# First backward steps of an attention-block gradient kernel: a V tile, the first dK, rows of e, the dw4 stores and some side jobs in other places

## The chip, the cores and the metric

The kernel runs on one core of one Trainium2 chip. The metric is the device time of one execution in microseconds (us). A core has a matrix engine (PE, with its weight loads shown as PEld), a vector engine (DVE), a scalar engine (ACT), GpSimd (POOL) and a queue engine (SP). They run side by side, each in its own program order, and wait for each other by semaphores. Transfers between HBM and on-chip memory are issued here from SP (nearly all loads), from POOL (all stores but a few at the end) and from ACT (small loads of rows of e); they share 16 DMA engines.

## What is computed

Forward and backward pass of one transformer block at decode: one token, attention over a cache of 8192 keys for 32 heads of 192, then a small MLP, each modulated by a vector from `c @ w_mod`. The kernel returns the output and the gradients of nine inputs. Cut to what matters:

```python
def attn(x, k, v, wq, wo):                  # 32 heads, 8192 keys, head size 192
    q = x @ wq
    p = softmax(q . k * 192**-0.5)
    return (p . v) @ wo
def mlp(x, w1, w2, w3, w4):                 # one token: only x, w3 and w4 matter
    x1 = x + hs
    return x1 + gelu(layernorm(x1) @ w3) @ w4
h = layernorm(x) * (1 + ca) + sa;  x = x + ga * attn(h, K, V, wq, wo)
h = layernorm(x) * (1 + cb) + sb;  x = x + gb * mlp(h, ...)
# outputs: x and the gradients of x, K, V, wq, wo, w3, w4, c, w_mod
```

K and V are 100 MB each in bfloat16 and so are their gradients dK and dV. Each row of dV is p times the gradient dO of a head's output, and each row of dK is dS times q, where dS comes from p and from dP, the products of dO with the rows of V. K is read once (forward), V twice (forward for the output, backward for dP), and dK and dV are written once.

## The kernel before

**Stages.** A forward loop over the heads loads K and V in tiles of 128 partitions x 32 rows x 192 (1536 KB, half a head) and leaves e (unnormalised p) in `E_all`, and transposed rows of e in DRAM (`eT_d`). The code after the loop handles the last head, the MLP forward and its backward down to `dao_bf`, the gradient at the attention output. Then come 64 backward steps `s` (L1363), one for each half head, from the last head down.

**Tiles.** Five tiles `KB` (names KX, KY, KC, KD, KE at L353) held K in the forward pass. In the backward pass the list `OB` (L354) gives them in turn to dV and dK: step `s` writes dV to `OL[2s]` and dK to `OL[2s+1]` (L1293). So dV of step 0 is in KC, dK of step 0 in KY, dV of step 1 in KX, dK of step 1 in KE, and so on round. Three tiles `VB` hold V; the V tile of step 0 was loaded to KY, those of steps 1 to 3 to VB2, VB0 and VB1 (`v_buf`, L1290) before the backward pass begins. The V tile of step 4 goes to VB2 again.

**One backward step.** DVE multiplies the V tile of the next step by dO, half a tile at a time (`mul_q`, L1035). PE sums the products with an identity matrix into `dot_ps` (`tree_q`, L1056), DVE reduces that to dP (`dot_sum`, L344) and forms dS. DVE multiplies dS by q, in two halves (`dk_part`, L1072), and POOL issues the store of dK (`dk_store`, L1322). For dV, PE forms the outer products of rows of e (`er_b`, loaded by `load_er`, L995) and dO in eight groups (`dv_groups`, L1067), ACT copies each from PSUM to the dV tile (L1068), and POOL issues the store (`dv_store`, L1318). SP loads the V tile of step s+4 as soon as the second half product of step s+1 has freed its tile (L1407). In steps 0 and 1 PE also forms dq from K tiles that are still there (`dq_rows`, `dq_cols`), and DVE waits for it before it starts dK.

**Before step 0.** A prelude (L1325 to L1360) does dV of step 0 and the products for steps 0 and 1. The gradient of w4 (dw4) is 12 blocks of 128x640, each the product of a broadcast row with a column (`dw4_dve` on DVE, `dw4_act` on ACT). Four blocks go to KX on DVE and are stored; five more go to another part of KX (three on DVE, two on ACT) and are stored; three go to the staging tile `stg0` on ACT and are stored. Three small pieces of work on DVE, kept in `late0` (L1362), run in step 0.

**Side jobs.** The gradients of wo, w3, wq and w_mod are cut into pieces (generators `g_do`, `g_dwo`, `g_ld`, `g_dw3`, `g_dq` and others). The list `jobs` (L1245) holds them in order, and `slot()`, called four times in a step, runs about one piece a call from step 6 on. `g_ld` loads a wo tile, `g_do` transposes it in two pieces and forms dO of two heads in the third, `g_dwo` overwrites it with the gradient and stores it. `g_dw3` forms rows of the gradient of w3 in the staging tile `stg` (a single buffer, so it waits for the store before) and stores them; the last one also loads the first wq chunk, over the tile from which `g_dw3` reads. `g_rest(3)` is three empty pieces.

**Order.** PE, DVE, ACT and SP run in an order that a planner fixes from the program's order (L355 and the `manual_schedule` blocks); POOL runs in the program's order.

Of the kernel before, what the change touches and what calls it, by code (L numbers as in the profile page):

```python
# [20 lines left out]
def kernel(  # L21
# [28 lines left out]
    D = A_x.shape[-1]  # L50
# [75 lines left out]
    def mean_sum(ps, groups, name):  # L126
        m = tcol(groups, name)
        V_.reduce_sum(out=m, in_=ps[:, 0 : groups * ND].rearrange("p (a b) -> p a b", b=ND), axis=AX.X)
        return m
# [187 lines left out]
    def flat(kb):  # L317
        return kb.rearrange("p j d -> p (j d)")


    NVB = 3
# [29 lines left out]
    H1 = HQ - 1  # L351
    TL = NT - 1
    KX, KY, KC, KD, KE = (KB[(2 * HQ + k) % NKB] for k in (-4, -5, -3, -2, -1))  # L353
    OB = (KC, KY, KX, KE, KD)  # L354
    NVA = (7 * JQ) // 16  # L355
    MO = 256
    with tc.tile_pool(name="vs", bufs=3) as vsp, tc.tile_pool(name="ft", bufs=2) as ft, \
# [85 lines left out]
        def mp_out(h, mp):  # L443
            A_.copy(out=M1[:, h, :], in_=mp[:, 0:MW])
            mt = ft.tile([P, MW], FP32, name="mt", bufs=1)
            A_.copy(out=mt[64:128, :], in_=mp[64:128, MO : MO + MW])
            return mt
# [8 lines left out]
        def m_add(h, mp, mt):  # L456
            t, b = divmod(h, 2)
            V_.tensor_tensor(out=M2[64 * b : 64 * b + 64, t, :], in0=mp[0:64, MO : MO + MW], in1=mt[64:128, :], op=ALU.add)
# [56 lines left out]
        with tc.manual_schedule(engines=ORDER):  # L515
# [297 lines left out]
            def w3t(n=1):  # L813
                for _ in range(n):
                    next(w3t_it, None)
# [56 lines left out]
            w3t()  # L872
            pe.pop(0)()
            w3t()
            dw4_v = out_7.rearrange("(a p) r -> p a r", p=P)

            def dw4_dve(dst, a0, lo, hi):
                for a in range(lo, hi):
                    V_.tensor_scalar(out=dst[:, (a - a0) * D : (a - a0 + 1) * D], in0=dbo_bc, scalar1=g_[:, a : a + 1], scalar2=None, op0=ALU.mult)

            def dw4_store(dst, lo, n):
                nc.gpsimd.dma_start(out=dw4_v[:, lo : lo + n, :], in_=dst[:, 0 : n * D].rearrange("p (a r) -> p a r", a=n))
# [24 lines left out]
                    T_.matmul(h2_ps[:, k : k + 1], lhsT=w4r(a)[:, k * P : (k + 1) * P], rhs=g_bf[:, a : a + 1], start=(a == 0), stop=(a == NF - 1))  # L907
            do_t(TL, 0)
            do_t(TL, 8)
            mt = mp_out(H1 - 1, mp)  # L910

            def dw4_act(dst, a0, lo, hi):
                for a in range(lo, hi):
                    A_.activation(out=dst[:, (a - a0) * D : (a - a0 + 1) * D], in_=dbo_bc, func=ACT.Copy, scale=g_[:, a : a + 1])

            dn_ps = psO.tile([P, 256], FP32, name="dn_ps", tag="op")[:, 0:ND]
            for k in range(ND):
                for a in range(NF):
                    T_.matmul(dn_ps[:, k : k + 1], lhsT=w3T(a, k), rhs=du_bf[:, a : a + 1], start=(a == 0), stop=(a == NF - 1))

            sk = mean_sum(ps5, 5, "sk")
            w6 = col(6 * ND, "w6").rearrange("p (a b) -> p a b", b=ND)
            A1, Ag, B1, Bg, uu, vv = (w6[:, k, :] for k in range(6))
# [6 lines left out]
            NWg = col(4 * ND, "NWg").rearrange("p (a b) -> p a b", b=ND)  # L930
            V_.tensor_scalar(out=NW, in0=NW, scalar1=rho[:, 0:1], scalar2=None, op0=ALU.mult)
            V_.tensor_copy(out=bo, in_=h2_ps[:, 0:ND])
            dw4_dve(flat(KX), 0, 0, 2)
            pr = col(4 * ND, "pr").rearrange("p (a b) -> p a b", b=ND)
            V_.tensor_tensor(out=pr, in0=dn_ps[:, None, :].to_broadcast([P, 4, ND]), in1=G, op=ALU.mult)
            ps = mean_mm(pr.rearrange("p a b -> p (a b)"), 4 * ND)
# [14 lines left out]
            V_.reduce_sum(out=qr, in_=q4.rearrange("p a b -> p b a"), axis=AX.X)  # L951
            V_.tensor_tensor(out=dao_bf, in0=vg, in1=qr, op=ALU.add)
            V_.tensor_copy(out=d_n2, in_=dn_ps)
            m_add(H1 - 1, mp, mt)
            dw4_dve(flat(KX), 0, 2, 4)
            dw4_store(flat(KX), 0, 4)

            def dx1_out():
                q = pr
# [38 lines left out]
    def ht(s):  # L998

        return H1 - s // 2, (1 - s % 2 if s < 2 else s % 2)  # L1000
# [46 lines left out]
    def half_q(s, q):  # L1047
        if halved(s, q):
            V_.tensor_tensor(out=pq[:, q, :, 0:HW], in0=pq[:, q, :, 0:HW], in1=pq[:, q, :, HW:DH], op=ALU.add)
# [63 lines left out]
    def g_do(n):  # L1113
        do_t(TL - n, 0)
        yield
        do_t(TL - n, 8)
        yield
        assert done_s[0] >= 4 * (n - NDR + 1)
        do_mm(TL - n)
        done.add(n)  # L1120
        yield
# [62 lines left out]
    def g_dwo(n):  # L1184
        t = TL - n
        w = wo_l.pop(t)
        for k in range(3):
            V_.tensor_scalar(out=w[:, k, :], in0=dao_bc, scalar1=o_col[:, 3 * t + k : 3 * t + k + 1], scalar2=None, op0=ALU.mult)
        nc.gpsimd.dma_start(out=dwo_v[t], in_=w)
        yield  # L1190

    def g_rest(n):
        for _ in range(n):
            yield
# [21 lines left out]
    def g_dw3(lo, n):  # L1216
        dw3_v = out_6.rearrange("(i p) n -> p i n", p=P)
        o3 = bst.tile([P, ND, CW], BF16, name="stg").rearrange("p a r -> p (a r)")
        for i in range(n):
            V_.tensor_scalar(out=o3[:, i * F : (i + 1) * F], in0=du_bc, scalar1=n2[:, lo + i : lo + i + 1], scalar2=None, op0=ALU.mult)  # L1220
        nc.gpsimd.dma_start(out=dw3_v[:, lo : lo + n, :], in_=o3[:, 0 : n * F].rearrange("p (a r) -> p a r", a=n))
        if lo + n == ND:
            next_w()
        yield
# [26 lines left out]
    late = list(range(GX, NWM))  # L1251
    for n in range(NT):
        if n + 3 < NT:
            jobs.append((3, g_do(n + 3)))
            if n < 2:
                jobs.append((1, g_dw3(2 * n + 2, 2 - n)))
            jobs.append((1, g_dwo(n + 3)))
        if n + 4 < NT:
            jobs.append((1, g_ld(n + 4)))
        if n == 1:  # L1260
            jobs.append((3, g_rest(3)))
        if n > 0:
            jobs.append((5, g_dq(TL - n + 1)))
            if n % 2 == 1:
                wseq.append((wq_v, (TL - n + 1) // 2))
        if n % 4 == 0 and n > 0 and late:
            wseq.append((wm_v, late[0]))
            jobs.append((10, g_wm(late.pop(0))))
# [19 lines left out]
            prog[1] += 1  # L1288

    def v_buf(s):  # L1290
        return KY if s == 0 else VB[(s + 1) % NVB]

    OL = [OB[i % 5] for i in range(2 * NS - 5)]  # L1293
    OL += [v_buf(NS - 3), OB[3], v_buf(NS - 2), OB[4], v_buf(NS - 1)]
# [36 lines left out]
    do_mm(TL, 0)  # L1331
    mul_q(0, 1)
    half_q(0, 1)
    dv_groups(dV0, er, doh, (4,))
    tree_q(ps, 0, 0, 0, 6)
    dv_groups(dV0, er, doh, (6,))
# [13 lines left out]
    T_.matmul(c_ps, lhsT=c32, rhs=cs, start=True, stop=True)  # L1350
    dv_groups(dV0, er, doh, (5, 7))
    dv_store(0, dV0, JQ, JH)
    dw4_dve(flat(KX)[:, 4 * D :], 4, 4, 7)
    dw4_act(flat(KX)[:, 4 * D :], 4, 7, 9)
    dw4_store(flat(KX)[:, 4 * D :], 4, 5)
    dw4_act(stg0[:, 2 * D :], 9, 9, 12)
    dw4_store(stg0[:, 2 * D :], 9, 3)
    V_.scalar_tensor_tensor(out=cpr, in0=c_ps, scalar=32.0, in1=rinv, op0=ALU.mult, op1=ALU.mult)
    V_.memset(dha, 0.0)
    V_.memset(dsc, 0.0)  # L1360
# [2 lines left out]
    for s in range(NS):  # L1363
        h, t = ht(s)
        nxt = s + 1 < NS
        doh = do_of(h)
        qh = qs_bc[:, h * DH : (h + 1) * DH]
        dP = tcol(JH, "dP")
        dot_sum(ps, dP)
        dS4 = bst.tile([P, JH, 4], BF16, name="dS4", bufs=2)  # L1370
        V_.scalar_tensor_tensor(
            out=dS4,
            in0=dP[:, :, None].to_broadcast([P, JH, 4]),
            scalar=cpr[:, h : h + 1],
            in1=E_all[:, h, t * JH : (t + 1) * JH, None].to_broadcast([P, JH, 4]),
            op0=ALU.subtract,
            op1=ALU.mult,
        )
        dV, dK = OL[2 * s], OL[2 * s + 1]
        gs = [0, 1, 2, 3, 4, 5, 6, 7]  # L1380
        if not nxt:
            gs = [0, 2, 4, 6, 1, 3, 5, 7]
        if s == 0:
            gs = [None] * 8
        else:
            er = er_l.pop(s)
        if nxt:
            ps = psR.tile([P, JH, TS], FP32, name="dot_ps")

        def dv(k):  # L1390
            if gs[k] is not None:
                dv_groups(dV, er, doh, (gs[k],))

        def tree(q, lo, hi):
            if nxt:
                tree_q(ps, s + 1, q, lo, hi)

        dv(0)
        dv(1)
        slot()  # L1400
        tree(0, 0, 4)
        if nxt:
            mul_q(s + 1, 1)
            half_q(s + 1, 1)
            v_l.pop(s + 1, None)
        if s + 4 < NS:
            v_l[s + 4] = load_v(*ht(s + 4), v_buf(s + 4))  # L1407
        dv(2)
        tree(0, 4, 8)
        dv(3)  # L1410
        tree(0, 8, 12)
        if row is not None:
            dq_cols(row)
            row = None
        dk_part(dK, qh, dS4, 0, JQ)
        if not nxt:
            dv_store(s, dV, 0, JQ, nc.sync)
            dk_store(s, dK, 0, JQ)
        slot()
        dv(4)  # L1420
        tree(1, 0, 3)
        dk_part(dK, qh, dS4, JQ, JH)
        while late0:
            late0.pop(0)()
        dk_store(s, dK, 0 if nxt else JQ, JH)
        dv(5)
        tree(1, 3, 6)
        slot()
        dv(6)
        tree(1, 6, 9)  # L1430
        dv(7)
        if s + 2 < NS:
            er_l[s + 2] = load_er(s + 2)
        if s == 0:
            pass
        elif nxt:
            dv_store(s, dV, 0, JH)
        else:
            dv_store(s, dV, JQ, JH, nc.sync)
        tree(1, 9, 12)  # L1440
        if h == H1:
            row = dq_rows(t, (KD, KE)[t], dS4)
        if s + 2 < NS:
            assert (s + 2) // 4 in done
            mul_q(s + 2, 0)
            half_q(s + 2, 0)
        done_s[0] = s + 1
        slot()
# [33 lines left out]
```

## Time and profile before

| what | us |
|---|---|
| median of 3 runs (1411.46 to 1414.79) | 1413.57 |
| the profiled execution | 1412.54 |
| its span, first to last instruction | 1410.8 |
| PE busy | 1182.7 (84%) |
| DVE busy | 1112.0 (79%) |
| ACT busy | 902.5 (64%) |
| POOL busy | 106.0 (8%) |
| mean rate of all transfers over the span | 404 GB/s |
| HBM read and written | 340.95 MB and 226.43 MB |

Times in the text are from the start of the profiled span. A line of the timeline gives the start, the duration, the engine, the line of the program, the operation with its tiles (buffer numbers left out, so KB is any of the five) and a count; in square brackets stands the idle time before it and what ended it. A line of the stretches gives the busy time of PE, PEld, DVE, ACT and POOL in that stretch with the number of instructions, then the granted clock of PE as a share of full speed, the mean busy share of the 16 DMA engines, and the rate. SPq and ACTq are DMA issues. Matmuls overlap, so a busy PE is not PE at its peak.

### The profile page before, as it was taken

How to read it: one execution, taken by the hardware profiler on the slowest of the kernel's cores; microseconds unless marked ns; L12 is line 12 of the kernel's file. 1: busy time of each engine (PE TensorE's matmuls, PEld its weight loads, DVE VectorE, ACT ScalarE, POOL GpSimd, SP SyncE). 2: the span in 40 equal slices, each digit the busy share in tenths (PEclk: the TensorE clock that was granted, in tenths of full speed). 3: DMA queues.
4: the chain of work that ended last, by engine and by line, in shares of the span. 5: the costliest groups of instructions: out<-in, count | busy, mean ns of one | idle time of the engine just before them, and what ended most of it. 6: DMA issues, size and time to landing. Idle time of an engine off the chain costs nothing.

```text
span 1410.8 us, 30413 instructions
## 1 busy us (share of the span) xinstructions
PE 1182.7 (84%) x12680; PEld 745.5 (53%) x12680; DVE 1112.0 (79%) x1461; ACT 902.5 (64%) x1971; POOL 106.0 (8%) x191
## 2 busy tenths in 40 slices
PE   3988989999998999797867998896877799878965
PEld 2777777777777778443323444443443344334421
DVE  4989999999999998886755875776775777868765
ACT  0767777777777778565545666665655476546654
POOL 0000000000000000110100111101110111101110
PEclk7899999999999999665555555556556555555555
DMA  9999999999999997599999999999999999999998
GB/s 375 389 398 419 418 416 423 411 422 417 418 415 415 408 416 291 209 365 427 424 388 424 427 422 426 421 425 425 425 421 425 414 413 426 419 404 396 424 369 373
DMA packets 76200, 569.36 MB, mean 404 GB/s; under 512 B 7294, under 2 KB 25038, under 8 KB 35998
## 3 DMA queue, kind: packets, MB, share of 16 engines
q1 hardware_dynamic: 51162, 342.03, 59.4%
q0 software_dynamic: 24384, 224.87, 38.3%
q8 instruction: 99, 1.62, 0.4%
q10 hardware_dynamic: 516, 0.51, 0.1%
q14 instruction: 39, 0.32, 0.1%
HBM read 340.95 MB, written 226.43 MB: 402 GB/s over the span
## 4 chain that ended last, share of the span: by engine, by line
issue 58%; DMA 17%; PE 9%; DVE 9%; POOL 5%; ACT 1%; SPq 0%; POOLq 0%; DVEq 0%; ACTq 0%
DMA KB<-in_A_k_cache_dram 7%; DVE prod L330 4%; DMA out_dram<-KB 3%; DMA w_st<-in_A_wq_dram 3%; PE mp L402 2%; DVE prod L334 2%; PE dot_ps L1056 2%; POOL out_dram L1322 2%; POOL out_dram L1318 2%; DMA out_dram<-w_st 2%; DMA stg<-in_A_wq_dram 2%; PE half_ps L340 2%; DMA out_dram<-stg 1%; PE mp L407 1%; PE dv_ps L1067 1%
## 5 line engine op out<-in xcount | busy, mean ns | idle before, releaser
L1068 ACT CAST KB<-dv_ps 128x768 bf16<-128x768 f32 x512 | 397.5, 805 | 164.1 <-PE dv_ps L1067 156.6
L1056 PE MATMUL dot_ps<-pq,ident_bf 128*128 128x256 bf16 x1494 | 380.3, 398 | 22.5 <-DVE dP L344 20.2
L1072 DVE TENSOR_TENSOR KB<-qs_bc,dS 128x3072 bf16<-128x3072 bf16 x122 | 210.7, 1753 | 131.8 <-DMA out_dram<-KB 124.6
L387 ACT ACTIVATE vs<-VB,Ef 128x192 bf16<-128x192 bf16 x840 | 303.5, 447 | 0.0
L1056 PEld LDWEIGHTS <-ident_bf 128*128 128x128 bf16 x1494 | 150.4, 124 | 177.6 <-issue 137.8
L1067 PE MATMUL dv_ps<-do_r,er_b 1*128 1x192 bf16 x2048 | 231.1, 337 | 9.5 <-ACT KB L1068 6.5
L1037 DVE TENSOR_TENSOR pq<-VB,do_r 128x3072 bf16<-128x3072 bf16 x126 | 220.4, 1749 | 15.4 <-PE dot_ps L1056 15.4
L330 DVE TENSOR_TENSOR prod<-KB,qs_bc 128x6144 bf16<-128x6144 bf16 x62 | 207.9, 3353 | 25.5 <-DMA KB<-in_A_k_cache_dram 19.8
L402 PE MATMUL mp<-vs,KB 128*128 128x193 bf16 x1984 | 191.2, 249 | 4.2 <-ACT vs L387 3.3
L402 PEld LDWEIGHTS <-KB 128*128 128x128 bf16 x1984 | 170.4, 98 | 13.3 <-DMA KB<-in_A_k_cache_dram 5.3
L894 ACT COPY wT<-wT_ps 128x1024 bf16<-128x1024 bf16 x82 | 79.1, 965 | 120.4 <-PE wT_ps L893 115.5
L1067 PEld LDWEIGHTS <-er_b 1*128 1x128 bf16 x2048 | 69.6, 104 | 161.1 <-issue 157.9
L340 PE MATMUL half_ps<-prod,ident_bf 128*128 128x256 bf16 x744 | 95.1, 279 | 44.2 <-DVE prod L334 44.1
L380 DVE TENSOR_TENSOR vs<-VB,E 128x1728 bf16<-128x1728 bf16 x120 | 123.7, 1052 | 0.3 <-ACT vs L387 0.3
L334 DVE TENSOR_TENSOR prod<-prod 128x3072 bf16<-128x3072 bf16 x62 | 108.7, 1754 | 1.0
L407 PE MATMUL mp<-vs,KB 128*64 128x193 bf16 x1976 | 107.2, 252 | 0.0
L340 PEld LDWEIGHTS <-ident_bf 128*128 128x128 bf16 x744 | 72.9, 100 | 62.4 <-issue 53.4
L344 DVE TENSOR_REDUCE dP<-dot_ps 128x32 f32<-128x512 f32 x64 | 44.0, 687 | 59.7 <-PE dot_ps L1056 59.5
L407 PEld LDWEIGHTS <-KB 128*64 128x64 bf16 x1976 | 80.1, 110 | 20.1 <-issue 19.7
L367 ACT ACTIVATE E<-S_h,negm 128x256 bf16<-128x256 f32 x31 | 15.8, 508 | 114.9 <-DVE negm L538 112.6
L1322 POOL DMA_DIRECT2D out_dram<-KB x61 | 33.6, 551 | 488.2 <-DVE KB L1072 300.4
L422 PE MATMUL op<-vs,ones_bf 128*32 128x193 bf16 x1920 | 62.1, 250 | 0.0
(359 smaller groups left out, 972.0 us busy)
## 6 DMA issues: line engine op xcount, KB each, us to landing
VB<-in_A_v_cache_dram SPq DMA_DIRECT2D x123, 1536.0 KB
out_dram<-KB POOLq DMA_DIRECT2D x123, 1536.0 KB, 16.1
KB<-in_A_k_cache_dram SPq DMA_DIRECT2D x64, 1536.0 KB
wo_st<-in_A_wo_dram SPq DMA_DIRECT2D x31, 480.0 KB
w_st<-in_A_wq_dram SPq DMA_DIRECT2D x12, 960.0 KB
out_dram<-wo_st POOLq DMA_DIRECT2D x16, 480.0 KB, 16.3
out_dram<-w_st POOLq DMA_DIRECT2D x7, 960.0 KB, 20.6
w_st<-in_w_mod_dram SPq DMA_DIRECT2D x6, 960.0 KB
```

The lines of the kernel that those rows point to most:

```text
L330: V_.tensor_tensor(out=prod, in0=src, in1=vec[:, None, :].to_broadcast([P, JH, DH]), op=ALU.mult)
L334: V_.tensor_tensor(out=prod[:, :, 0:HW], in0=prod[:, :, 0:HW], in1=prod[:, :, DH - HW : DH], op=ALU.add)
L340: T_.matmul(ps, lhsT=ident_bf, rhs=prod[:, :, k : k + TF], start=(k == 0), stop=(k == w - TF))
L380: V_.tensor_tensor(out=vs[:, 0:n, 0:DH].rearrange("p j (a b) -> p j a b", b=4), in0=v[:, v0 : v0 + n, :].rearrange("p j (a b) -> p j a b", ...
L387: A_.activation(out=vs[:, k, 0:DH], in_=v[:, v0 + k, :], func=ACT.Copy, scale=Ef[:, j0 + k : j0 + k + 1])
L402: T_.matmul(mp[:, 0:MW], lhsT=kb[:, j0 + k, 0:P], rhs=vs[:, k, 0:MW], start=(q == 0 and k == 0), stop=(z and k == JQ - 1), skip_group_chec ...
L407: T_.matmul(mp[p0 : p0 + 64, MO : MO + MW], lhsT=kb[:, j0 + k, P:DH], rhs=vs[:, k, 0:MW], start=False, stop=(z and k >= JQ - 2), skip_grou ...
L1037: V_.tensor_tensor(out=pq[:, q], in0=v_l[s][:, q * JQ : (q + 1) * JQ, :], in1=do_of(ht(s)[0])[:, None, :].to_broadcast([P, JQ, DH]), op=AL ...
L1056: T_.matmul(ps[:, q * JQ : (q + 1) * JQ, :], lhsT=ident_bf, rhs=pq[:, q, :, k : k + TS], start=(k == 0), stop=(k == w - TS), skip_group_ch ...
L1067: T_.matmul(ps[:, b, k * DH : (k + 1) * DH], lhsT=er[p0 : p0 + 1, 2 * m + k, :], rhs=doh[p0 : p0 + 1, :], start=True, stop=True)
L1068: A_.copy(out=dV4[:, 2 * q : 2 * q + 2, m * PW : (m + 1) * PW], in_=ps[:, :, 0:PW])
L1072: V_.tensor_tensor(out=dK[:, lo:hi, :].rearrange("p j (a b) -> p j a b", b=4), in0=qh.rearrange("p (a b) -> p a b", b=4)[:, None, :, :].to ...
```

## The change

- `OB`: the second of the five output tiles is VB2 in place of KY. So dK of step 0 is written to VB2, and VB2 goes round among the output tiles. KY takes VB2's place among the V tiles: the V tile of step 4 is loaded to KY, and its load is issued in the prelude, after the second half product of step 0, no longer in step 0's body after the second half product of step 1.
- `mp_out` and `m_add` of the next-to-last head (two copies on ACT, one addition on DVE) are done sooner. They are among the last readers and writers of tiles in whose memory `er_b` comes to lie, so the first load of rows of e waited for the addition.
- dw4: six blocks on DVE, all in KX (three before `pr`, three after `d_n2`), in one store; six blocks on ACT, all in `stg0`, in one store. Three stores become two, and DVE does six blocks in place of seven.
- `late0`: one piece in each of steps 1, 2 and 3, not all three in step 0.
- side jobs: `g_dw3(2, 2)` and `g_dw3(4, 1)` each three pieces sooner; with the latter goes the load of the first wq chunk. `g_rest(3)` now stands between them and `g_do(4)`, so `g_do(4)` comes four pieces later, and `g_dwo(4)` and the wo load `g_ld(5)` three pieces later. The number of pieces is the same.

```diff
-    OB = (KC, KY, KX, KE, KD)
+    OB = (KC, VB[2], KX, KE, KD)
...
             w3t()
             pe.pop(0)()
             w3t()
+            mt = mp_out(H1 - 1, mp)
...
             do_t(TL, 0)
             do_t(TL, 8)
-            mt = mp_out(H1 - 1, mp)
...
+            m_add(H1 - 1, mp, mt)
             sk = mean_sum(ps5, 5, "sk")
...
-            dw4_dve(flat(KX), 0, 0, 2)
+            dw4_dve(flat(KX), 0, 0, 3)
...
             V_.tensor_copy(out=d_n2, in_=dn_ps)
-            m_add(H1 - 1, mp, mt)
-            dw4_dve(flat(KX), 0, 2, 4)
-            dw4_store(flat(KX), 0, 4)
+            dw4_dve(flat(KX), 0, 3, 6)
+            dw4_store(flat(KX), 0, 6)
...
         if n + 3 < NT:
-            jobs.append((3, g_do(n + 3)))
             if n < 2:
                 jobs.append((1, g_dw3(2 * n + 2, 2 - n)))
+            if n == 1:
+                jobs.append((3, g_rest(3)))
+            jobs.append((3, g_do(n + 3)))
             jobs.append((1, g_dwo(n + 3)))
         if n + 4 < NT:
             jobs.append((1, g_ld(n + 4)))
-        if n == 1:
-            jobs.append((3, g_rest(3)))
...
     def v_buf(s):
-        return KY if s == 0 else VB[(s + 1) % NVB]
+        return KY if s == 0 else VB[2] if s == 1 else (VB[1], KY, VB[0])[s % 3]
...
     half_q(0, 1)
+    v_l[4] = load_v(*ht(4), v_buf(4))
...
     dv_store(0, dV0, JQ, JH)
-    dw4_dve(flat(KX)[:, 4 * D :], 4, 4, 7)
-    dw4_act(flat(KX)[:, 4 * D :], 4, 7, 9)
-    dw4_store(flat(KX)[:, 4 * D :], 4, 5)
-    dw4_act(stg0[:, 2 * D :], 9, 9, 12)
-    dw4_store(stg0[:, 2 * D :], 9, 3)
+    dw4_act(stg0, 6, 6, 12)
+    dw4_store(stg0, 6, 6)
...
-        if s + 4 < NS:
+        if 0 < s < NS - 4:
             v_l[s + 4] = load_v(*ht(s + 4), v_buf(s + 4))
...
-        while late0:
+        if s > 0 and late0:
             late0.pop(0)()
```

## The prediction

> **What bounds the kernel now.** I read the 40 slices of the page, then stretches around the turn from forward to backward, the chain of waits, and the timelines of the engines there.
>
> ```profile
> DMA  9999999999999997599999999999999999999998
> GB/s 375 389 398 419 418 416 423 411 422 417 418 415 415 408 416 291 209 365 427 424 388 424 427 422 426 421 425 425 425 421 425 414 413 426 419 404 396 424 369 373
> ```
>
> The transfers bound nearly all of it; one hole stands in slices 16 to 18 (529 to 635 us).
>
> ```profile
> 574.00:584.00 10.00, 8.59 (x57) 4.47 (x58) 9.83 (x17) 6.55 (x10) 0.54 (x1) 0.50 0.38 145
> 584.00:602.00 18.00, 12.42 (x103) 7.50 (x101) 12.68 (x23) 8.25 (x12) 2.79 (x4) 0.59 0.94 357
> 602.00:608.00 6.00, 5.97 (x67) 3.38 (x66) 4.97 (x5) 3.82 (x7) 1.08 (x2) 0.50 0.72 301
> 608.00:618.00 10.00, 7.94 (x71) 4.32 (x70) 6.79 (x8) 8.36 (x14) 1.07 (x2) 0.94 0.98 374
> 618.00:640.00 22.00, 21.36 (x134) 8.42 (x135) 18.49 (x18) 14.52 (x19) 2.68 (x5) 0.53 1.00 386
> 640.00:720.00 80.00, 55.17 (x350) 24.09 (x351) 50.27 (x59) 39.16 (x54) 9.50 (x17) 0.54 1.01 425
> 724.00:726.00 2.00, 2.00 (x14) 0.85 (x15) 2.00 (x3) 1.99 (x3) 0.20 (x1) 0.50 0.77 324
> ```
>
> The last columns are granted clock, DMA share and rate. From 640 transfers are the limit; before 618 computing decides when they can start. By windows of 2 us the missing shares from 574 to 618 add up to 9.7 us (2 x (1 - share) each): 7.4 before 586, 1.9 to 608, 0.4 after. Moving computing sooner pays only in as far as it fills these.
>
> ```profile
> 585.59 10.96 DMA out_dram<-KB
> 605.95 1.40 PE dq_ps L1304 x26
> ```
>
> In the chain, a store of KB (the second dw4 store) is followed by PE's work of step 1: that store sets the pace.
>
> ```profile
> 572.25 1.14 SPq L995 DMA_DIRECT2D er_b<-eT_d  x2
> 584.93 9.93 SPq L325 DMA_DIRECT2D VB<-in_A_v_cache_dram  x2
> ...
> 575.13 0.82 PE L1067 MATMUL dv_ps<-do_r,er_b 1*128 1x192 bf16 x8 [2.37 <-DVE pq L1037]
> 581.15 0.97 DVE L879 TENSOR_SCALAR KB<-w4b,g__10304 128x640 bf16<-128x640 bf16 x3
> 588.16 0.16 DVE L1362 SCALAR_TENSOR_TENSOR du<-t__10307,d_g 128x12 f32<-128x12 f32 x1
> 590.09 1.75 DVE L1037 TENSOR_TENSOR pq<-VB,do_r 128x3072 bf16<-128x3072 bf16 x1
> 596.65 2.24 ACT L1068 CAST KB<-dv_ps 128x768 bf16<-128x768 f32 x3 [6.32 <-DMA out_dram<-KB]
> 597.50 0.50 PE L1067 MATMUL dv_ps<-do_r,er_b 1*128 1x192 bf16 x4 [2.60 <-ACT KB L1068]
> 616.26 0.53 POOL L1322 DMA_DIRECT2D out_dram<-KB  x1 [9.40 <-DVE KB L1072]
> 719.82 1.04 PE L893 MATMUL wT_ps<-ident_bf,wo_st 128*128 128x128 bf16 x8 [13.00 <-DMA wo_st<-in_A_wo_dram]
> ```
>
> **The chain to the store of dK of step 2 (616.26), term by term.**
>
> *Moved out of the way.* ACT's two copies of `mp` (0.34 + 0.32) fall into its idle 1.23 before 568.07; without that cover the wT copies, done at 569.89, still have 1.9 until do_ps starts. On DVE the addition (0.35) and a third dw4 block (0.34) come before `pr`, where DVE waits 0.57 for dn_ps: 0.12 late. Afterwards three blocks (0.97) replace the addition and two (1.03). Taken: 0.
>
> *Rows of e.* The first load then waits for the last matmul of dn_ps, near 569.9, in place of the addition that ended at 572.18. It took 2.9 from issue to PE's start at 575.13, so it lands near 572.8 and dO, ready at 573.23, decides. PE's first tree needs the halved product (DVE, 576.01), so at most 1.2 of it arrives there (577.24), at least 0. Taken: 0.8, near the middle of the higher part, since PE has its groups behind it by then; c_ps (581.41 to 581.88) ends at 581.1.
>
> *Three dw4 blocks less on DVE at 581.15.* They took 0.97. Without them DVE is free at 581.24, and with c_ps at 581.1 the next operation (cpr, 582.04) starts at 581.3: -0.75. Were c_ps not sooner, it would be -0.1.
>
> *late0.* 590.09 - 588.16 = 1.93 leaves step 0. The reduction to dP at 591.76 comes 0.75 + 1.93 = 2.7 sooner; PE's tree before it, ended at 588.2, is 0.75 sooner too and stays ahead. It returns as 0.1 in step 1, 0.8 in step 2 and 1.1 in step 3, each behind that step's dK.
>
> *KX.* ACT's 6.32 before dV of step 1 was the store issued at 585.59, landing after 11.0. Now KX's only store leaves at 573.2; the four blocks took 3.7 to land there, in an emptier queue. For six the bounds are 3.7 and 11.0, so 584.2 at the latest, and ACT comes there at about 588.7 (PE's first groups of step 1, 589.16, less the 0.75). ACT's sixth block (0.74) is covered by its idle 1.83 before 589.28. PE's 2.60 goes: -2.6.
>
> Sum: 0.75 + 1.93 + 2.6 = 5.3 sooner. Step 2's dK is stored near 611.
>
> *The tiles.* VB2 is free for dK of step 0 when the second product of step 1 is done, just before on DVE. Five output and three V tiles remain: 0 from then on.
>
> *The transfers.* SP idles from 573 on, so the V load moves from 584.93 to about 577.7, 7.2 sooner, into the hole: 1.57 MB, 3.7 at 425 GB/s. The second dw4 store, six blocks on ACT from 583.0, leaves at 587.5 (583.0 + 6 x 0.745), as before (587.74), and dK of step 0 behind it on POOL's queue (588.54) too. What nothing fills is the time before the V load (about 2) and before that dw4 store (some 2.5): about 4.7 stays of 9.7, with the lag of some 1.4 from an issue to a rising share. So transfers allow 5.0 and computing 5.3. Some waste will stay between: I take 4.7, bounds 0.5 (below) and 5.3.
>
> **The side jobs.** At 706.8 PE waits 13.0 for the wo tile loaded just ahead of `g_do(4)`. With four pieces between (a step, about 13) that wait goes. The DMA share falls short by 0.96 at 722 to 726, after it. Bounds: 0, and 3.0 if all of 720 to 740 (356 and 367 GB/s) rose to 425. Taken: 0.7.
>
> The price is a new wait. `g_dw3(2, 2)` needs the single `stg`, whose store was issued at 674.34 and lands after 19.8, at 694.1; DVE now reaches the piece near 688.6 and waits up to 5.5. Behind it stand a product, so PE's tree and the next V load on SP, and dK. `g_dw3(4, 1)` may meet the same with its own predecessor: up to 6. They cost only what runs dry: a dK or dV store lands 16.1 after its issue and needs 3.7 itself, so 12.4 are queued, and the 13.0 wait above cost 0.96. Bounds 0 and 11.5; taken 0.4. The wq chunk (960 KB, 2.3) goes ahead of one V load on SP, and wo loads later; V is loaded three steps ahead, so nothing. PE's 8.6 wait for that chunk at 753 goes, under a share of 1.0: nothing.
>
> Sum: 4.7 + 0.7 - 0.4 = 5.0. Span 1410.8 - 5.0 = 1405.8; the profiled execution is 1.74 above its span, and the median 1.03 above that: 1413.57 - 5.0 = 1408.6.
>
> **The clock.** PE's work is priced at the granted clock of these rows, about 0.53. The Trainium skill's page TensorE: Matmul & The Clock Gate, Part 1, says that a busy window of about 3.4 us brings the full clock; with PE's gap closed, step 1 would run at 1.0. Here it does not hold: 618 to 640 PE is 97% busy at 0.53. By the rule PE would gain some 5 more, but the transfers cap it: 1408.3 against 1408.6.
>
> **Rivals.**
>
> *PE's pace takes it back.* 608 to 618 ran at a clock of 0.94 with 5.94 of PE work; sooner, it may get 0.53, where it takes 10.5, 4.6 more, partly under the wait for dq_c; say 3. And PE is the limit from 618 to 640 (21.36 of 22), so late0's 1.9 in steps 2 and 3 may come back. Then 5.3 - 4.8 = 0.5 stays of the chain: 1413.57 - 0.5 - 0.3 = 1412.8. For it: the full clock came just there. Against it: from 618 the DMA share is 1.0, so there the pace is not PE's alone.
>
> *Slower: the staging tile.* If the two waits for `stg` in `g_dw3` (5.5 and 6) run the queues dry, 11.5 - 4.7 - 0.7 = 6.1 is lost: 1419.7. It decides from where a wait exceeds the 12.4 queued, or both fall together. For it: V loads stop with DVE. Against it: the 13.0 wait cost 0.96.
>
> *More.* All of the dip at 720 to 740 goes: 4.7 + 3.0 = 7.7, 1405.9. Against it: small rows of w3 and wq go there anyway.
>
> That the change leaves the er load where it was is possible too (another wait ends last); it takes 0.8 of the forecast at most and stays in its range.
>
> **Chances.** Forecast 0.61 (own range 1407.0 to 1410.7), more 0.10, PE's pace 0.17, staging tile 0.12. About 0.2% (2.8 us) is what a measurement can tell here. Faster 0.71, same 0.17, slower 0.12. The range leaves out the slower case and some of "more": 1405.0 to 1414.0.
>
> **What would show it.** Right: er_b issued near 570; a V load near 577.7; no ACT wait for a store before dV of step 1; dP of step 1 near 589, dK of step 2 stored near 611; DMA share over 0.9 from 602 to 608; no wait of PE for wo_st near 710. Wrong: a clock near 0.5 in step 2 with that store after 614; DVE waiting over 5 at L1220 with a DMA share under 0.9 behind it; or a saving at 640 that is lost by 760.

## The result, and the profile after

The changed kernel takes 1406.81 us (median of 9 runs, 1403.01 to 1410.15), the kernel before on the same chip 1412.49 (9 runs, 1409.40 to 1415.95). The ratio is 0.996 with an interval of 0.9944 to 0.9977: 5.7 us less. The forecast was 5.0 us less, 1408.6.

The profiled executions differ by only 2.4 us (1412.54 and 1410.14), because the forward part, whose program is the same, happened to run 3.3 us longer in the second. So from here on times are also given from a common mark: the start of DVE's operation that writes `du_bf` (L869), with which the MLP backward begins. It starts at 567.44 before and at 570.74 after; from it to the end of the span it is 1410.8 - 567.44 = 843.36 and 1408.4 - 570.74 = 837.66, 5.7 less. To compare a time of after with one of before, take 3.3 off.

The DMA share and the rate in 40 slices, from the page of after:

```profile
DMA  9999999999999998599999999999999999999998
GB/s 375 396 393 419 419 405 419 416 419 417 422 413 416 400 408 327 202 386 427 421 420 425 426 424 421 421 425 412 426 417 424 417 419 414 404 412 391 423 396 355
```

The low pair of shares 7 5 (slices 16 and 17) is now 8 5, and the low rate of slice 21 (388) is 420.

Stretches of after that answer to those of before, each 3.3 us later; the last columns are granted clock, DMA share and GB/s:

```profile
577.30:587.30 10.00, 8.85 (x57) 4.63 (x53) 9.83 (x14) 7.24 (x11) 1.13 (x3) 0.50 0.78 246
587.30:605.30 18.00, 16.98 (x167) 10.28 (x166) 15.78 (x16) 12.60 (x18) 2.45 (x4) 0.59 0.95 360
605.30:611.30 6.00, 5.58 (x40) 2.88 (x38) 1.70 (x4) 3.69 (x7) 0.00 (x0) 0.73 1.02 432
611.30:621.30 10.00, 8.34 (x59) 3.69 (x56) 9.83 (x16) 6.47 (x10) 1.61 (x3) 0.53 0.96 403
...
727.30:729.30 2.00, 2.00 (x18) 1.01 (x17) 0.01 (x1) 1.74 (x4) 0.00 (x0) 0.83 1.05 435
```

The first stretch goes from a share of 0.50 to 0.78 (145 to 246 GB/s), the third from 0.72 to 1.02 (301 to 432), and the last, the dip behind PE's long wait, from 0.77 to 1.05. PE's busy time in 18 us rises from 12.42 to 16.98: most of its idle time in step 1 is gone. Summed as in the prediction (2 us windows, 2 x (1 - share)), from 6 to 74 us after the mark 10.9 us were missing before and 5.3 are after.

The timelines of after, around the same places:

```profile
573.13 1.12 SPq L995 DMA_DIRECT2D er_b<-eT_d  x2
581.23 0.35 SPq L325 DMA_DIRECT2D KB<-in_A_v_cache_dram  x1
...
576.80 0.82 PE L1067 MATMUL dv_ps<-do_r,er_b 1*128 1x192 bf16 x8 [0.51 <-ACT do_r L1021]
592.46 0.68 DVE L344 TENSOR_REDUCE dP<-dot_ps 128x32 f32<-128x512 f32 x1
592.23 1.50 ACT L1068 CAST KB<-dv_ps 128x768 bf16<-128x768 f32 x2
594.10 1.61 ACT L1068 CAST KB<-dv_ps 128x768 bf16<-128x768 f32 x2 [0.37 <-PE dv_ps L1067]
596.38 0.16 DVE L1313 TENSOR_TENSOR dq_x<-dq_c,dq_x 128x1 f32<-128x1 f32 x1 [1.19 <-PE dq_c L1312]
600.47 0.53 POOL L1322 DMA_DIRECT2D out_dram<-KB  x1 [8.01 <-DVE KB L1072]
609.85 0.16 DVE L1313 TENSOR_TENSOR dq_x<-dq_c,dq_x 128x1 f32<-128x1 f32 x1 [4.25 <-PE dq_c L1312]
614.24 0.53 POOL L1322 DMA_DIRECT2D out_dram<-KB  x1 [10.52 <-DVE pr L960]
...
692.20 1.15 DVE L1220 TENSOR_SCALAR stg<-w4b,nQ 128x1536 bf16<-128x1536 bf16 x2 [5.28 <-DMA out_dram<-stg]
721.12 1.04 PE L894 MATMUL wT_ps<-ident_bf,wo_st 128*128 128x128 bf16 x8 [3.26 <-DMA wo_st<-in_A_wo_dram]
758.17 1.03 PE L894 MATMUL wT_ps<-ident_bf,wo_st 128*128 128x128 bf16 x8 [7.03 <-DMA wo_st<-in_A_wo_dram]
```

Rows of e leave at 569.83 on the clock of before. ACT's copies of dV of step 1 (592.23, 594.10) wait for PE at most; the 6.32 for a store is gone. dK of step 1 is stored 29.73 after the mark (36.18 before), dK of step 2 43.50 after it (48.82 before). PE's 13.00 for the wo tile has become 3.26 and, one tile later, 7.03 (10.3 together), and DVE waits 5.28 for the store of `stg`.

### The profile page after: what moved, and what is told of

It is laid out like the page before. It is cut to its first block, busy times and chain, and to the rows that moved or that the text cites. A ratio compares the mean times of both kernels' runs of the same rounds, so it can differ in the third digit from the quotient of the medians.

```text
span 1408.4 us, 30414 instructions
## 1 busy us (share of the span) xinstructions
PE 1184.5 (84%) x12680; PEld 746.2 (53%) x12680; DVE 1111.7 (79%) x1460; ACT 903.4 (64%) x1972; POOL 104.9 (7%) x190
## 3 DMA queue, kind: packets, MB, share of 16 engines
q0 software_dynamic: 24368, 224.87, 38.4%
## 4 chain that ended last, share of the span: by engine, by line
issue 30%; DMA 25%; DVE 22%; PE 17%; POOL 4%; ACT 1%; SPq 0%; POOLq 0%; DVEq 0%
DMA KB<-in_A_k_cache_dram 11%; DVE prod L330 8%; DVE prod L334 4%; PE mp L402 3%; PE dot_ps L1056 3%; DMA stg<-in_A_wq_dram 3%; DMA w_st<-in_A_wq_dram 3%; DMA out_dram<-KB 3%; DVE vs L380 2%; PE half_ps L340 2%; DMA w_st<-in_w_mod_dram 2%; PE mp L407 2%; DVE pq L1037 2%; PE dv_ps L1067 2%; POOL out_dram L1322 1%
## 5 line engine op out<-in xcount | busy, mean ns | idle before, releaser
L1068 ACT CAST KB<-dv_ps 128x768 bf16<-128x768 f32 x416 | 321.8, 803 | 112.0 <-PE dv_ps L1067 110.7
L1072 DVE TENSOR_TENSOR KB<-qs_bc,dS 128x3072 bf16<-128x3072 bf16 x98 | 169.4, 1753 | 104.5 <-DMA out_dram<-KB 100.2
L1037 DVE TENSOR_TENSOR pq<-VB,do_r 128x3072 bf16<-128x3072 bf16 x86 | 150.5, 1750 | 7.9 <-PE dot_ps L1056 6.2
L1068 ACT CAST VB<-dv_ps 128x768 bf16<-128x768 f32 x96 | 75.1, 802 | 38.2 <-PE dv_ps L1067 38.0
L1037 DVE TENSOR_TENSOR pq<-KB,do_r 128x3072 bf16<-128x3072 bf16 x42 | 73.5, 1751 | 5.7 <-PE dot_ps L1056 5.1
```

Of the source, the lines that this page charges most:

```text
L1037: V_.tensor_tensor(out=pq[:, q], in0=v_l[s][:, q * JQ : (q + 1) * JQ, :], in1=do_of(ht(s)[0])[:, None, :].to_broadcast([P, JQ, DH]), op=AL ...
L1068: A_.copy(out=dV4[:, 2 * q : 2 * q + 2, m * PW : (m + 1) * PW], in_=ps[:, :, 0:PW])
L1072: V_.tensor_tensor(out=dK[:, lo:hi, :].rearrange("p j (a b) -> p j a b", b=4), in0=qh.rearrange("p (a b) -> p a b", b=4)[:, None, :, :].to ...
```

## The experiments

Each profile is read by three times from the mark: the store of dK of step 2, and when 250 and 300 MB of the 569 MB have moved (the rates of stretches of 4 us, summed). The table has them beside the times; each median stands against that of the kernel before on the same chip. The three times from the mark come from one profiled execution of each kernel, the median from all its executions.

| kernel | median us | kernel before | ratio, interval | dK of step 2 | 250 MB | 300 MB |
|---|---|---|---|---|---|---|
| before | | 1412.49 | | 48.82 | 72.5 | 192.9 |
| changed | 1406.81 | 1412.49 | 0.9944 to 0.9977 | 43.50 | 67.2 | 185.2 |
| e1, first steps | 1404.21 | 1411.16 | 0.9942 to 0.9967 | 38.35 | 65.7 | 186.2 |
| e2, jobs | 1411.68 | 1411.16 | 0.999 to 1.0015 | 48.19 | 71.9 | 189.7 |
| e3, V tile alone | 1409.6, one run | 1411.16 | | 46.71 | 70.5 | 190.2 |
| e4, later V load in the program | 1404.13, one run | 1411.16 | | 41.91 | 65.2 | 186.5 |
| e5, first steps, old tiles | 1406.11 | 1411.87 | 0.9946 to 0.9977 | 43.48 | 67.4 | 189.0 |
| e6, first steps, old dw4 | 1407.55 | 1411.87 | 0.9958 to 0.9986 | 44.27 | 68.0 | 188.3 |
| e7, changed again | 1406.51 | 1411.87 | 0.9949 to 0.9982 | 41.92 | 65.2 | 183.7 |
| e8, first steps, dq after dK | 1406.66 | 1411.87 | 0.9952 to 0.9992 | 36.48 | 65.5 | 184.8 |
| e9, dw4 alone | 1409.91 | 1412.06 | 0.9971 to 0.9996 | 45.79 | 69.3 | 190.9 |
| e10, late0 alone | 1412.41 | 1412.06 | 0.9997 to 1.0026 | 47.74 | 71.5 | 193.2 |
| e11, dw4 and late0 | 1408.23 | 1412.06 | 0.9957 to 0.9981 | 38.77 | 66.7 | 187.2 |
| e12, first steps and wo tile | 1405.81 | 1412.06 | 0.9939 to 0.9973 | 41.90 | 65.3 | 184.1 |

In the eleven profiles in which dK of step 2 is stored later than 41 us after the mark, 250 MB follow it by 23.3 to 23.9 us, from 41.9 and 65.2 to 48.8 and 72.5. In the other three (36.5 to 38.8) they stay at 65.5 to 66.7. So over these profiles the transfers keep step with that store one for one down to about 42, and below it not at all. And in all twelve experiments (e3 and e4 are single runs) the time fell by what 250 MB were sooner, to within 2 us; in ten of them it fell by less.

### The two halves of the change: e1 and e2

e1 is the changed kernel with the side jobs in their old order; e2 is the kernel before with the new order alone:

```diff
-            jobs.append((3, g_do(n + 3)))
...
+            if n == 1:
+                jobs.append((3, g_rest(3)))
+            jobs.append((3, g_do(n + 3)))
...
-        if n == 1:
-            jobs.append((3, g_rest(3)))
```

> The changed kernel with the side jobs in their old order. Progress is the time from the start of du_bf (L869) until so many MB have been moved in all: 250 MB at 72.5 us before and 67.2 in the changed kernel, 300 MB at 192.9 and 185.2. Theory (the first steps and the jobs each bring a part of their own): 250 MB at 67.2, but 300 MB only at about 187.6 (the first steps' 5.3 and no more), PE waits some 13 us for a wo tile again, and the median is 4 to 6 us below before. Rival (the prediction's small share for the jobs): 300 MB within 1 us of 186. Rival (the first steps' gain is lost by itself later): 300 MB above 190 and a median no different from before.

> The kernel before with only the side jobs in the new order. Theory: nothing moves up to 250 MB (72.5 us from du_bf), the PE wait for wo_st of 13 us goes, and 300 MB are moved at 190.5 in place of 192.9, 2.4 sooner; the median falls by about 2 us, which its scatter may hide. Rival (the prediction's term, 0.7 less 0.4): 192.6. Rival (the wait for the staging tile costs): DVE waits over 4 us before the second g_dw3 and 300 MB come after 193.

e1 takes 7.0 us off, e2 nothing (0.5 more, inside its interval). So the gain is in the first steps; for the jobs alone no gain is measured. The waits of e2 between 690 and 800 us (engine and line, what is waited for: us in total, times, longest):

```profile
PE wT_ps L893 <- DMA wo_st<-in_A_wo_dram: 12.3, 2, 6.9
...
DVE stg L1220 <- DMA out_dram<-stg: 5.5, 1, 5.5
```

The one wait of 13.0 became two of 6.9 at most (12.3 together), and the dip after it went: 300 MB move 3.2 us sooner than before (189.7 against 192.9), though 250 MB only 0.6. So the job order takes the dip near 150 us after the mark away. In this profile 400 MB move 2.1 us later than before, but it shows the slowest of e2's twelve executions (1417.60, median 1411.68), so it doesn't show that the job order itself loses the gain again.

### The tiles of V: e3, e4, e5

e3 is the kernel before with only the other tiles and the V load in the prelude. e4 is e1 without the load's new place in the program (it stays behind the product of step 1). e5 is e1 with the tiles as before:

```diff
-    OB = (KC, VB[2], KX, KE, KD)
+    OB = (KC, KY, KX, KE, KD)
...
-    v_l[4] = load_v(*ht(4), v_buf(4))
```

> The kernel before with only the tiles exchanged and the V load of step 4 in the prelude. Theory (computing decides when transfers can go on, up to the store of dK of step 2): that store stays near 48.8 us from du_bf, and 250 MB come at 72 to 72.5, a gain of 0.5 at most, though the V load itself is issued about 7 us sooner. Rival (the hole in the transfers alone counts): 1.57 MB are moved into the hole, so 250 MB come 3.7 us sooner, at 68.8.

> The changed kernel's first steps with the new tiles, old order of the side jobs, but the V load of step 4 issued in step 0's body as before. Theory (two limits, computing and the filling of the hole, both needed): the store of dK of step 2 stays near 43.5 us from du_bf, yet 250 MB come at 69 to 71, later than 67.2 by the 3.7 us of that load less what idle time is left behind 586. Rival (computing alone decides): 250 MB at 67.2 to 67.7.

> The changed kernel's first steps and the old order of the side jobs, but dK of step 0 in KY and the V tile of step 4 in VB2 as before, so that its load waits for the second product of step 1: issued near 16.7 us from the start of du_bf, not 10.5. Two runs with the new tiles had 250 MB at 65.7 and 65.2 us. Theory (the filling of the hole counts as well as computing): the store of dK of step 2 stays at 38 to 43.5, idle time of the transfers up to 18 us from du_bf is near 6 us, not 3, and 250 MB come at 67.5 to 69.5; the median is some 2 us above the run with the side jobs alone undone (1404.2). Rival (computing alone): 250 MB at 65 to 67 and no difference.

e4 missed its aim: the load was issued 10.5 us after the mark, as in the changed kernel, wherever it stands in the program. It is one more look at the first steps.

e3 did neither of the two things expected: it gained 2.0 us at 250 MB, by a way that I had not seen. The DMA issues between 568 and 600 us (KB each, median us from issue to landing), first of the kernel before:

```profile
out_dram<-KB POOLq DMA_DIRECT2D x1, 800.0 KB, 11.0
```

and of e3, with ACT's wait for that store from its timeline:

```profile
out_dram<-KB POOLq DMA_DIRECT2D x1, 800.0 KB, 6.2
```

```profile
589.61 0.80 ACT L1068 CAST KB<-dv_ps 128x768 bf16<-128x768 f32 x1 [1.35 <-DMA out_dram<-KB]
```

It is the second dw4 store from KX, for whose landing ACT waited 6.32 before. Before, SP issued a V load of 1536 KB at 584.93, just ahead of that store (585.59). With the V load gone from there the store lands in 6.2 in place of 11.0, and ACT waits 1.35.

e5 turns it round. Without the tiles the hole at 6 to 18 us after the mark stays (6.4 us missing in place of 3.1) and 235 MB are moved 0.9 us later than in the changed kernel, but 250 MB only 0.2 later, in an execution whose clock and dK stores are the same (43.48 and 43.50): by the MB moved, later stretches take nearly all of what the hole did not. (By the shares they give back less: 0.8 missing from 18 to 74 us in place of 2.2.) The time gains 5.8 us all the same; e1, with the tiles, gained 7.0, and the intervals don't tell the two apart.

### dw4 and late0: e6, e9, e10, e11

e6 is e1 with dw4 in its old three stores. e9 is the kernel before with dw4 in two stores alone, e10 with `late0` put off alone, e11 with both and nothing else:

```diff
-    dw4_dve(flat(KX)[:, 4 * D :], 4, 4, 7)
-    dw4_act(flat(KX)[:, 4 * D :], 4, 7, 9)
-    dw4_store(flat(KX)[:, 4 * D :], 4, 5)
-    dw4_act(stg0[:, 2 * D :], 9, 9, 12)
-    dw4_store(stg0[:, 2 * D :], 9, 3)
+    dw4_act(stg0, 6, 6, 12)
+    dw4_store(stg0, 6, 6)
...
-        while late0:
+        if s > 0 and late0:
```

> The changed kernel's first steps and the old order of the side jobs, but dw4 in three stores as before (the second one out of KX, three more blocks on DVE). Theory (the wait for KX's store was the largest term): ACT waits again before dV of step 1, though less than 6.3 us, since with the V load sooner that store lands sooner (1.35 in the run with the V load alone); dK of step 2 is stored 0.8 to 3.4 later than the 38 to 43.5 us of the other runs, and 250 MB come at 67 to 69. Rival (transfers cap everything): 250 MB at 65 to 66 still.

> The kernel before with dw4 in two stores alone. If the chain of computing sets when step 2's dK is stored, ACT's wait of 6.3 us for the store of KX goes and 2.6 us of PE's idle time with it: dK of step 2 is stored 46 to 46.5 us after the start of du_bf (before 48.8), 250 MB are moved 70 to 71.5 us after it (before 72.5), and the time falls by 1 to 2 us. Rival, the place of the V load decides: it stays behind the dw4 store, so 250 MB stay within 0.5 us of 72.5 and the time within 0.7 us.

> The kernel before with the late vector work of step 0 put off to steps 1 to 3, alone. By the chain dP of step 1 comes 1.9 us sooner, but ACT's wait for the store of KX grows from 6.3 to about 8.2 us, so dK of step 2 stays near 48.8 us after the start of du_bf, 250 MB near 72.5, and the time within 0.7 us of before. Rival, each term counts by itself: dK of step 2 near 46.9, 250 MB near 70.6, 1.9 us less.

> Both together: dw4 in two stores and step 0's late vector work put off; V tile, rows of e and jobs as before. By the chain 2.6 + 1.9 us: dK of step 2 near 44.3 us after the start of du_bf, 250 MB 68 to 69, the time 3.5 to 4.5 us less. Rival, the V load's place sets what transfers can gain: dK of step 2 as sooner, but 250 MB not under 70.5 and the time 2 us less at most.

e9: the wait for KX is gone, dK of step 2 is 3.0 us sooner and 250 MB 3.2 us, and the time falls by 2.2. e6, the same edit taken out of the whole: 250 MB and dK of step 2 each 0.8 us later than in the changed kernel, which like e6 has only short spells of full clock there. At 250 MB the edit is worth 3 alone and about 1 among the others, since the earlier V load takes most of the same wait away (in e6 too the 800 KB land in 6.2, and ACT has no wait for a store before dV of step 1).

e10: dP of step 1 comes 1.95 us sooner (22.37 after the mark, before 24.32), about the 1.93 that was moved, and half of it stops at KX. ACT's line in its timeline:

```profile
594.92 2.24 ACT L1068 CAST KB<-dv_ps 128x768 bf16<-128x768 f32 x3 [6.01 <-DMA out_dram<-KB]
```

ACT still waits 6.01 for the store, until 28.3 after the mark (before 29.2). 250 MB move 1.0 us sooner, between the two expectations, and the time does not show it (0.35 more, inside its interval).

e11: together they give 5.8 us at 250 MB, more than the 3.2 and 1.0 apart, and 3.8 us of time against 2.2 and -0.35, a difference inside the intervals. The profiles don't settle it either: dK of step 2 was expected near 44.3 and came at 38.77, in an execution with 17.1 us of full clock in these steps, where e9's had 6.8 and e10's 3.4. That the two edits give more together than apart is therefore not shown. Of stretches of 4 us of e11, two before the V load, which SP issues at 583.22, and one of the steps after it:

```profile
576.00:580.00 4.00, 4.00 (x26) 1.64 (x23) 3.67 (x6) 2.88 (x4) 0.55 (x1) 0.50 0.27 110
580.00:584.00 4.00, 3.84 (x25) 2.58 (x24) 3.64 (x7) 3.35 (x6) 0.54 (x1) 0.50 0.37 146
592.00:596.00 4.00, 4.00 (x69) 2.42 (x68) 4.00 (x4) 4.00 (x6) 0.48 (x1) 1.00 1.04 431
```

The hole before the V load (shares 0.27 and 0.37) is all there, and still 250 MB are moved at 66.7, 1.0 us later than in e1, whose full clock lasted as long. So most of the gain at 250 MB comes from when the steps' results come, which the KX wait held up; the V load in the hole and the sooner rows of e are worth about that 1.0 there. In time e1 gained 3.2 us more than e11 (7.0 and 3.8), with intervals that overlap, so what they are worth in the end stays open.

### What caps it: e8, and the changed kernel again, e7

In the changed kernel DVE waits 4.25 for dq before dK of step 2 (609.85). e8 is e1 with that moved behind dK:

```diff
-        if row is not None:
-            dq_cols(row)
-            row = None
         dk_part(dK, qh, dS4, 0, JQ)
...
+        if row is not None:
+            dq_cols(row)
+            row = None
         if s > 0 and late0:
```

> The changed kernel's first steps, side jobs in the old order, and in steps 0 to 2 the columns of dq (dq_cols) taken after dK, no longer before it, so that DVE doesn't wait there for PE (1.2 and 4.3 us in the changed kernel, 0.6 and 0.6 where PE had its full clock). Theory: dK of steps 1 and 2 is stored up to 4 us sooner where PE is at half clock, but the transfers lie idle for only 1.3 us between 18 and 40 us from du_bf, so 250 MB come at 64 to 65.5 and the median gains 1 us at most. Rival (nothing left to gain): 250 MB at 65.2 or later.

> The changed kernel again, on the chip and against the same runs of the kernel before as the others of this batch, for a second profile. Theory (the new order of the side jobs saves 2 to 3 us near 160 us from du_bf and gives them back later): a median 1 to 3 us above that of the run with the first steps alone, 300 MB at 183 to 185.5 us from du_bf, and more than 2 us lost against 425 GB/s somewhere between 200 and 500 us, where that run lost 2.3. Rival (that loss was chance): a median at or below 1404.2, under 2.5 us lost there.

The store of dK of step 2 in the timelines of e8 and of e7:

```profile
602.10 0.53 POOL L1322 DMA_DIRECT2D out_dram<-KB  x1 [5.86 <-DVE KB L1072]
```

```profile
607.68 0.53 POOL L1322 DMA_DIRECT2D out_dram<-KB  x1 [9.23 <-DVE pr L960]
```

The marks are 565.62 and 565.76. e8 stores dK of step 2 at 36.5, seven us sooner than the changed kernel's profile, and no wait for dq is left in steps 1 and 2. Not all of the seven is the edit: against e1, which like e8 ran most of these steps at the full clock, it is 1.9. 250 MB are moved at 65.5 and the time is no shorter than that of e1. In e7 dK of step 2 comes at 41.9 and 250 MB at 65.2, no later than in any other run. So nothing was won by storing dK of step 2 sooner than that.

### One job alone: e12

All first steps, and of the jobs only `g_rest(3)` ahead of `g_do(4)`, so that the wo tile has its time; dw3's rows and the wq chunk stay in their places.

```diff
+            if n == 1:
+                jobs.append((3, g_rest(3)))
             jobs.append((3, g_do(n + 3)))
...
-        if n == 1:
-            jobs.append((3, g_rest(3)))
```

> All first steps of the change, and of the jobs only the wo tile's loads ahead of g_do(4); dw3 rows and the wq chunk in their old places. If the loss near 160 us after du_bf (about 2 us against 425 GB/s) goes and the later loss of the new order belongs to the dw3 rows or the wq chunk, the time falls below that of the first steps alone, to 1401.5 to 1403. Rival, the transfers give it back later whichever job is moved: 1404 to 1406, no dip near 160 us and some 2 us more lost from 200 to 500 us.

PE's waits for tiles of the side jobs in e12, from its timeline:

```profile
711.79 1.03 PE L894 MATMUL wT_ps<-ident_bf,wo_st 128*128 128x128 bf16 x8 [4.90 <-DMA wo_st<-in_A_wo_dram]
742.33 1.18 PE L894 MATMUL wT_ps<-ident_bf,w_st 128*128 128x128 bf16 x11 [9.88 <-DMA w_st<-in_A_wq_dram]
```

The wait for wo falls from e1's 14.65 to 4.90 and the rate behind it holds (424 and 420 GB/s from 140 to 160 us after the mark; in e1 399 and 331). No wait of DVE for `stg` is left. 300 MB move 2.1 us sooner than in e1, but the time is 6.3 us under that of before, where e1 had 7.0: nothing gained in the median, though the profiled execution was the fastest of its ten (1402.17). The median is what the rival expected (1404 to 1406), but the loss that it put from 200 to 500 us is hardly in the profile: e12 loses 2.1 there against 425 GB/s and e1 1.7, and from the mark to its end e12's execution is 3.6 us shorter than e1's (834.9 and 838.5). So neither a gain of this job nor its loss later is shown.

No version was found that is better than the changed kernel beyond doubt. e1 has the lowest median, and its interval (0.9942 to 0.9967) overlaps with that of the changed kernel.

## Why the prediction was right, point by point

**The hole.** That transfers bound all but one hole, and that computing sooner pays only until they are the limit, held. Some 4.7 us were to stay missing; 5.3 did, and 5.6 went (of 10.9, in windows that begin 0.6 us sooner and end later than those of the prediction), beside 5.7 of time.

**The chain to dK of step 2.** Forecast 5.3, measured 48.82 - 43.50 = 5.32. So close a match is luck: e7, the same kernel again, stores it at 41.92, which is 6.9 sooner than before. By terms:

| term | forecast | measured in after's profile |
|---|---|---|
| rows of e issued | near 569.9 | 569.83 |
| `cpr` and what lies before it | 0.75 | 14.60 - 13.93 = 0.67 |
| to dP of step 1, with late0 | 2.7 | 24.32 - 21.72 = 2.60 |
| the KX wait, to the store of dK of step 1 | 2.6 | 36.18 - 29.73 - 2.60 = 3.85 |
| given back before dK of step 2 | 0 | 6.45 - 5.32 = 1.13 |

Two terms were mis-sized and partly cancel. For KX I counted the one idle time of PE shown before 597.50 (2.60). But in the two stretches around it, 8 us, PE worked only 4.21 (busy time is the second number):

```profile
591.30:595.30 4.00, 2.41 (x12) 1.06 (x12) 3.16 (x4) 0.00 (x0) 0.00 (x0) 0.60 0.99 387
595.30:599.30 4.00, 1.80 (x12) 1.29 (x11) 0.00 (x0) 2.24 (x3) 0.00 (x0) 0.50 1.03 436
```

That is 3.8 idle, and DVE, which must have dq from PE before dK of step 1, waited for all of it; its line in the timeline of before, and the store of dK of step 1:

```profile
599.53 0.16 DVE L1313 TENSOR_TENSOR dq_x<-dq_c,dq_x 128x1 f32<-128x1 f32 x1 [5.03 <-PE dq_c L1312]
...
603.62 0.55 POOL L1322 DMA_DIRECT2D out_dram<-KB  x1 [14.50 <-DVE KB L1072]
```

These 5.03 became 1.19 (596.38 of after): 3.84, the whole term. The 1.1 given back is the same wait in step 2, 3.13 before and 4.25 after: PE's pace, a quarter of the 4.8 that the rival of that name gave it, though the clock fell to 0.53 at that place as the rival said. In e7, where a spell of full clock lay there, that wait is 2.97 and nothing is given back.

**What held KX.** The prediction named the store's late issue as the cause, which was part of it. The other part is the V load issued 0.66 us ahead of that store: without it the store lands in 6.2 in place of 11.0 and ACT waits 1.35 in place of 6.32 (e3). So the edits are not a sum: the V tile and the dw4 stores each take away most of one wait, and of late0's 1.95 only about half gets past that wait while it stands (e10). The prediction counted the wait once, as PE's idle time, which kept its sum from counting both edits; that its size came out as well is the luck named above.

**The V load into the hole.** The prediction let the transfers gain because the V load moves 7.2 us sooner into the hole. The move came (577.93 on the clock of before, forecast 577.7), but as the main reason it failed: e5 and e11 have no V load in the hole and gain 5.1 and 5.8 us at 250 MB. What the transfers gain in these profiles is what dK of step 2 gains, until it comes at about 42 us.

**The side jobs.** The 13.0 wait was to go; it came back as 3.26 and 7.03 (in e2 as 12.3 together). What the forecast had counted was the dip behind it, and that went. DVE's wait for `stg` is 5.28 (up to 5.5 forecast), and it has no dip behind it either. The gain near there was 7.7 - 5.3 = 2.4 us at 300 MB, not 0.7: the rival "more" was right for that dip. But in the time the jobs show no gain by themselves (e2), and with the first steps 7.0 without them stands against 5.7 and 5.4 with them, a difference inside the intervals. So the forecast's two parts, 4.7 for the first steps and 0.3 for the jobs, were measured alone as 7.0 us less (e1, interval 4.7 to 8.2) and 0.5 more (e2, from 1.4 less to 2.1 more): the first was probably too low, and 5.0 against 5.7 owes something to that. Against 425 GB/s the stretch from 200 to 500 us after the mark loses 2.4, 4.5 and 7.1 us with the new order (after, e7, e2) and 0.6 to 2.4 in the old. after and e7 are the same kernel and e2's is its slowest execution, so that the new order costs this is not shown.

**The slower rival** did not come: no two waits for `stg` fell together, and 5.28 of DVE's time ran no queue dry (the DMA share is 1.00 to 1.03 in the 12 us behind 690).

## What to carry to other kernels

When several edits act before the same wait, find out what holds it (a late store, and what was issued ahead of that store) and count the wait once: each edit alone may give little or nearly all. Where transfers bound a kernel, measure an edit by the time at which a fixed amount has moved since a common mark, not by the span alone: a few us come and go in parts of the program that are the same. And a load that fills a hole gains little if later holes would have taken it; what counted most here is when the results came that had yet to be stored. Where the clock differs between two executions, a point in the middle of a chain can differ by several us in the same program, so compare such points at the same clock.

## What the runs showed of the hardware

The granted clock differs between executions at the same place of the same instructions. Stretches of 4 us from 22 to 34 us after the mark, first of the changed kernel, then of e1, whose first steps are the same program:

```profile
592.70:596.70 4.00, 3.50 (x29) 2.50 (x29) 2.76 (x5) 2.63 (x4) 0.00 (x0) 0.77 1.04 388
596.70:600.70 4.00, 4.00 (x31) 2.14 (x29) 3.97 (x5) 2.65 (x4) 0.23 (x1) 0.50 1.02 329
600.70:604.70 4.00, 3.97 (x55) 2.05 (x52) 3.04 (x4) 2.51 (x5) 0.84 (x2) 0.50 0.96 390
```

```profile
585.90:589.90 4.00, 3.58 (x39) 2.40 (x38) 3.34 (x6) 2.49 (x4) 0.00 (x0) 1.00 1.04 385
589.90:593.90 4.00, 3.88 (x67) 2.28 (x65) 4.00 (x4) 4.00 (x6) 0.53 (x1) 1.00 1.01 335
593.90:597.90 4.00, 3.64 (x33) 2.24 (x32) 3.34 (x5) 3.86 (x8) 0.53 (x1) 1.00 1.00 349
```

In e1, e8 and e11 the full clock lasts 17.1, 20.5 and 17.1 us without a break; after and e5 have two spells of 3.4, e7 and e12 two of 6.8. Among after, e7, e1 and e12, whose first steps are the same program, dK of step 2 moves between 38.4 and 43.5 with it, and 250 MB only between 65.2 and 67.2. In all fourteen traces the granted clock has no value but 0.5 and 1.0, and every spell but the last lasts a multiple of 3.41 us. The Trainium skill's page TensorE: Matmul & The Clock Gate, Part 1, says that the clock rises after a busy window of about 3.4 us and that the window runs freely, so that it falls differently in each run. The second part agrees with these rows. The first is half borne out: the prediction said that it does not hold here, and e1 shows that it can, while after stays at 0.50 through 8 us in which PE is 99% busy (7.97 of 596.70 to 604.70). The traces show what goes with a rise. Take the windows of 3.41 us at 0.5 in the 700 us behind the mark, in all fourteen. In each of the 144 after which the clock rises, matmuls other than the outer products of dV (`dv_ps`, marked `1*128` in the timeline, a single row) are busy for at least 80% of the window. Of the 2225 others only 205 reach that, though PE is at least 99% busy in 1203. No run here changes the share of those outer products, so that they are the cause is not shown.
